# An attention and FFN kernel: the third bank of a score group to VectorE, and two row blocks in FFN at once

## The chip, the cores and the metric

The kernel runs on one core of one Trainium2 chip. The metric is device time in microseconds, from a median of runs. A core has five engines with queues of their own: TensorE (PE; its weight loads are shown apart as PEld), VectorE (DVE), ScalarE (ACT), GpSimd (POOL) and SyncE (SP), which issues the transfers here. An engine works its queue off in order; what must wait for another engine waits on a semaphore. TensorE writes to PSUM, which has eight banks of 128 x 512 float32 values.

## What is computed

Two identical layers, each an attention part and an FFN part, over 2048 rows of 448 values. There are 16 heads of 28 values.

```python
x = A_x
for layer in range(2):                       # written out twice in the reference
    n = layernorm(x)                         # mean and variance over 448, eps 1e-5
    q, k, v = split(n @ wqkv)                # 16 heads, 28 values each
    p = softmax(q @ k.T * 28 ** -0.5)        # 2048 x 2048 for each head
    x = x + merge(p @ v) @ wo
    n = layernorm(x)
    h = maximum(n @ w1 + b1, 0) ** 2         # 1792 hidden values
    x = x + h @ w2 + b2
```

The exponentials are the largest part of the work outside TensorE: 2 layers x 16 heads x 2048 x 2048 values, which are 2048 tiles of 128 x 512.

## The kernel before

The Python code holds a small planner: each stream of work yields operations with an engine, an estimated duration and what they depend on, and the planner decides the order in which every engine's instructions are issued. So a change of a rule in it moves instructions everywhere. The parts that matter here follow.

Scores are made in groups of three tiles. A group has a PSUM tile of three banks ("sc", two buffers, so six banks). The other two banks of PSUM ("m") are shared by everything else: a fourth score tile of a group, the projections, the transposes, both FFN products, and attention times values.

```python
ps_sc = ctx.enter_context(tc.tile_pool(name="ps_sc", bufs=2, space=bass.MemoryType.PSUM))
ps_m = [ctx.enter_context(tc.tile_pool(name=f"ps_m{i}", bufs=1, space=bass.MemoryType.PSUM)) for i in range(2)]
```

ScalarE does the exponential of a whole group in one instruction, and gives the group's PSUM tile back when that has ended:

```python
pt = gbuf[gi]["pt"] = ptp.tile([P, 3 * 512], DT.bfloat16, name="pt")
nc.scalar.activation(out=pt[:, 0:n], in_=gbuf[gi]["sc"][:, 0:n], func=AF.Exp,
                     scale=float(np.log(2.0)) * 2.0 ** -FRAC)
```

Some groups have a fourth tile, in a shared bank. Its exponential is computed on VectorE, in six instructions: a first one that adds, clamps and converts to integers, and so empties the bank; then the fraction's polynomial and the power of two, from SBUF:

```python
nc.vector.tensor_scalar(out=box["i"], in0=two(src), scalar1=EXP_BIAS,
                        scalar2=EXP_LOW, op0=ALU.add, op1=ALU.max)          # empties the bank
...  # cut: three scalar_tensor_tensor for the polynomial, one tensor_scalar for the power
nc.vector.scalar_tensor_tensor(out=box["two"](pd), in0=box["h"], scalar=b0,
                               in1=box["e"].bitcast(DT.bfloat16), op0=ALU.add, op1=ALU.mult)
```

Whether a group gets a fourth tile is decided when it is issued. The last condition of `apart` asks for a free shared bank:

```python
if pl.load(SPAN, "DVE") > (BB if ... else BUSY):        # cut: VectorE too full in the last 12 us
    return None
near = p_next[0] is not None and e_now[0] >= p_next[0] - NEAR_U
want[0] = sum(r.when() is not None and r.when() <= now for r in R_m) < 1 + near
return None if want[0] else j
```

TensorE repeats score matmuls where there is room before the next work, to stay busy (line 753 holds both the first making and the repeats):

```python
short = (HOT if len(units) - at[0] > ENDU else HOTE) - pl.load(HWIN)
...  # cut
for i in list(range(4)) * (again + 1):
    for k, (pi, kb, r, hh) in enumerate(us):
        nc.tensor.matmul(dst[k][:, i * nt * P:(i + 1) * nt * P], lhsT=K_sb[l][rows, g, ...], rhs=Q_sb[rows, g, ...], ...)
```

When all four head groups of a row block (256 rows; the last one of layer 1 is two of 128) are done, a chain takes it through the projection with `wo`, the addition to `x`, layer normalization, the two FFN products with relu and square between them, and, in layer 0, on to the keys, values and queries of layer 1. In layer 0, one row block at a time may hold hidden activations; they lie in a pool of seven buffers:

```python
hp = ctx.enter_context(tc.tile_pool(name="hp", bufs=NFC // 2))     # 7
R_h = [Res(1), Res(2)]                                             # row blocks with activations, by layer

def hidden(i):
    if l == 0:
        return hp.tile([P, QB], DT.bfloat16, name="h")
    c = NFC * QR * (own_h.turn % 2) + QB * i
    return V_sb[0][:, :, :, :].rearrange("p t h r -> p (t h r)")[:, c:c + QB]
```

Of the kernel before, what the change touches and what calls it, by code (L numbers as in the profile page):

```python
# [11 lines left out]
DT = mybir.dt  # L12
AF = mybir.ActivationFunctionType
ALU = mybir.AluOpType
# [20 lines left out]
DCLK = 0.2  # L35
OWN = 2
HALF = 320
BB = 0.95
TURNS = 1
ENDU = 100  # L40
HOTE = 0.8
# [5 lines left out]
GATE = [None, None, ('Q', 0, 0, 0), ('Q', 0, 0, 0), ('s', 8), ('s', 8), ('s', 8), ('s', 8)]  # L47
EARLY = 2
AHEAD = (range(0, 4), range(0, 4), range(0, 4))
SLACK = 0.6  # L50
WINDOW = 2.8
C_PRIO = 1.5
V_PRIO = 6.0
# [19 lines left out]
HOLD = 5  # L73
HOLD1 = 7
SOON = 0.6
NL = 0
NLP = 3.8
STOP = 80
# [34 lines left out]
class Planner:  # L113
# [3 lines left out]
    def __init__(self):  # L117
        self.clock = {"PE": 0.0, "ACT": 0.0, "DVE": 0.0, "POOL": 0.0, "DMA": 0.0, "-": 0.0}
        self.mode = None
        self.tok = {}  # L120
        self.streams = []
        self.past = {"PE": [], "DVE": []}
        self.turns = lambda: False

    def load(self, span, eng="PE"):

# [33 lines left out]
    def run(self):  # L160
        while self.streams:
            cands = []
            for st in self.streams:
                s, e = self.earliest(st[2]) if st[2] is not None else (None, None)
                if s is not None:
                    cands.append((s, st[0](s) if callable(st[0]) else st[0], e, st))
            assert cands, "no stream can go on"
            known = cands

            due = next((c[3][2].ready for c in cands if c[1] == 0), None)  # L170
            if due is None:
                due = next((c[0] + c[3][2].dur + LAT["ACT"] for c in cands if c[1] == 1), None)
            if due is not None:
                ok = [c for c in cands if c[2] != "PE" or c[1] == 0 or c[0] + c[3][2].dur <= due + SLACK]
                cands = ok or cands
            s, _, e, st = min(cands, key=lambda c: (max(c[3][2].ready, self.clock[c[2]]) if c[2] == "PE" and self.turns() else c[0], c[1]))
            o = st[2]
            o.eng = (e,)
            if o.acq:
                o.res = min((r for r in (o.acq() if callable(o.acq) else o.acq) if r.when() is not None), key=lambda r: r.when())  # L180
                o.turn = len(o.res.rel)
                o.res.rel.append(None)
            o.start, o.end = s, s + o.dur
            if e == "PE":
                o.room = min([c[0] for c in known if c[2] == "PE" and c[3] is not st] or [1e9]) - o.end
            if o.fn:
                o.fn(e)
            o.end += o.more
            self.clock[e] = o.end - (OVER if e == "DVE" and o.dur > 0.1 else 0.0)
            if e == "PE":  # L190
                self.mode = o.mode
            if e in self.past:
                self.past[e] = [p for p in self.past[e] if p[1] > s - 40.0] + [(s, max(s, self.clock[e]))]
            for a in o.rel:
                a.got.append(o.end + o.lat + LAT[e])
                if len(a.got) == a.need:
                    a.res.rel[a.turn] = max(a.got)
            for key in o.sets:
                self.tok[key] = o
            st[2] = next(st[1], None)  # L200
            if st[2] is None:
                self.streams.remove(st)
# [3 lines left out]
def kernel(  # L206
# [28 lines left out]
    const = ctx.enter_context(tc.tile_pool(name="const", bufs=1))  # L235
    ptp = ctx.enter_context(tc.tile_pool(name="ptp", bufs=NPT))
    xtp = ctx.enter_context(tc.tile_pool(name="xtp", bufs=3))
    hp = ctx.enter_context(tc.tile_pool(name="hp", bufs=NFC // 2))
    rp = ctx.enter_context(tc.tile_pool(name="rp", bufs=2))
    vp = ctx.enter_context(tc.tile_pool(name="vp", bufs=1))  # L240
    osp = ctx.enter_context(tc.tile_pool(name="osp", bufs=NOS))
# [7 lines left out]
    pl = Planner()  # L249
    R_sc, R_m, R_pt = Res(2), (Res(1), Res(1)), Res(NPT)  # L250
    R_r, R_xt, R_os, R_xn, R_on, R_rec = Res(2), Res(3), Res(NOS), Res(2), Res(2), Res(2)
    R_h = [Res(1), Res(2)]

    R_v = (Res(1), Res(1))


    R_pd = [*[Res(1) for _ in range(5)], Res(NFC // 2), *[Res(1) for _ in range(2)]]


    x_sb = const.tile([P, NTB, D], DT.bfloat16, name="x_sb")  # L260
# [61 lines left out]
    def late_setup():  # L322
# [14 lines left out]
        yield Op("POOL", 0.2, lambda e: nc.gpsimd.memset(ones[:], 1.0))  # L337
        yield Op("POOL", 0.2, lambda e: nc.gpsimd.memset(one0[:], 0.0))
        yield Op("POOL", 0.2, lambda e: nc.gpsimd.memset(one0[0:1, :], 1.0))
        yield Op("POOL", 0.8, lambda e: nc.gpsimd.memset(V_sb[1][:, 0:12, :, DH:DHP], 1.0))  # L340

    def loads():
        kb = 1024
# [47 lines left out]
    def spare(n):  # L391


        def f():
            if s_left and (want[0] or p_next[0] is not None and e_now[0] >= p_next[0] - (NEAR if n < 8 else FAR)):
                return R_m if all(r.when() is not None for r in R_m) else ()
            return pools_now()
        return f

    p_next = [None]  # L400
    e_now = [0, 0]
    want = [False]

    def engs_now(early=False):
        return ("ACT", "DVE") if (early and ("s", AEND) not in pl.tok) or len(s_left) == 0 else ("DVE",)

    s_left = [True]
    pl.turns = lambda: TURNS == 2 or TURNS == 1 and len(s_left) == 0

    def moments():  # L410
# [139 lines left out]
    def qkv(l, t0, nt, xnT, own_xt, ends, early=False):  # L550
# [13 lines left out]
        def values():  # L564
            nonlocal last
            for tb in range(t0, t0 + nt):
                if l == 1 and tb >= 12:
                    yield Op("POOL", 0.2, lambda e, tb=tb: nc.gpsimd.memset(V_sb[1][:, tb, :, DH:DHP], 1.0))
                def evv(e, t, tb=tb):
                    o = V_sb[l][:, tb, :, 0:DH]  # L570
# [86 lines left out]

    taken = set()
    held = [0]

    def sets_of(unit):

# [3 lines left out]
            return R_v if 2 <= qb <= 6 else R_v[:1]  # L666
        return R_v

    def apart(i, now, us):


        want[0] = False
        if len(units) - i < STOP or not LEAD <= len(gbuf) <= LAST:
            return None
        l, qb = passes[units[i][0]][:2]
        if not any(r.when() is not None and r.when() <= now + SOON for r in sets_of(units[i])):
            return None
        j = i
        if i + LAG > ends_at[units[i][0]]:
# [11 lines left out]
            return None  # L691
        if pl.load(SPAN, "DVE") > (BB if l == 0 and qb == len(blocks[0]) - 1 or l == 1 and units[i][0] < bridged else BUSY):
            return None
        near = p_next[0] is not None and e_now[0] >= p_next[0] - NEAR_U
        want[0] = sum(r.when() is not None and r.when() <= now for r in R_m) < 1 + near
        return None if want[0] else j

    def ahead(n):

# [8 lines left out]
    def s_stream():  # L708
        while at[0] < len(units):
# [5 lines left out]
            def fn(e, gi=gi, us=us, js=js):  # L715
                sc = ps_sc.tile([P, 3 * 512], DT.float32, name="sc", tag="sc")
                gbuf[gi]["sc"] = sc
                dst = [sc[:, k * 512:k * 512 + 512] for k in range(len(us))]
                at[0] = js[-1] + 1
                rest = ahead(1)  # L720
                at[0] = rest[0] if rest else len(units)
                j = apart(at[0], o.start, us) if rest else None
                if j is not None:
                    us = us + [units[j]]
                    taken.add(j)
                    held[0] += 1
                    rest = ahead(1)
                    at[0] = rest[0] if rest else len(units)
                    x = gbuf[gi]["x"] = Op("PE", 0.0, None)
                    x.res = min((r for r in R_m if r.when() is not None), key=lambda r: r.when())  # L730
                    x.turn = len(x.res.rel)
                    x.res.rel.append(None)
                    dst.append(bank(x, "mt"))
                    pl.spawn(C_PRIO, a_unit(gi, x, dst[-1], us[-1], passes[us[0][0]][0]))
                for k, (pi, kb, r, hh) in enumerate(us):
                    where.setdefault((pi, kb), []).append((gi, k, hh))
                    if len(where[pi, kb]) == G:
                        pl.tok["u", pi, kb] = o
# [74 lines left out]
    def a_unit(gi, x, src, unit, l):  # L813
# [2 lines left out]
        box = {}  # L816

        def take(e):
            box["i"], box["h"], box["e"], two = set_of(c.res, l)
            box["two"] = two  # L820
            halves = box["i"].bitcast(DT.uint16).rearrange("p a (n t) -> p a n t", t=2)
            box["f"] = halves[:, :, :, 0]
            box["n"] = box["i"].bitcast(DT.int16).rearrange("p a (n t) -> p a n t", t=2)[:, :, :, 1]
            nc.vector.tensor_scalar(out=box["i"], in0=two(src), scalar1=EXP_BIAS,  # L824
                                    scalar2=EXP_LOW, op0=ALU.add, op1=ALU.max)
# [182 lines left out]
    def chain(l, qb):  # L1008
# [16 lines left out]
        hacts = []  # L1025

        def hidden(i):
            if l == 0:
                return hp.tile([P, QB], DT.bfloat16, name="h")

            c = NFC * QR * (own_h.turn % 2) + QB * i
            return V_sb[0][:, :, :, :].rearrange("p t h r -> p (t h r)")[:, c:c + QB]
        for f0 in range(0, NFC, pack):
            fcs = range(f0, min(f0 + pack, NFC))
            w = len(fcs) * n
# [6 lines left out]
                else:  # L1042
                    nc.vector.tensor_scalar(out=r[:, 0:w], in0=t[:, 0:w], scalar1=0.0, scalar2=None, op0=ALU.max)  # L1043
            def square(e, b=b, w=w, f0=f0):
                r = b["r"]
                b["h"] = h = hidden(f0 // pack)
                nc.vector.tensor_tensor(out=h[:, 0:w], in0=r[:, 0:w], in1=r[:, 0:w], op=ALU.mult)

            def then(o, b=b, square=square):
                b["s"] = Op("DVE", 0.42, square, deps=[o], rel=o)  # L1050
# [3 lines left out]
                 for i, fc in enumerate(fcs)],  # L1054
                relu, 0.70, [*ends, ("w1",)], True, post=[then], acq=R_r)
            for i in range(len(fcs)):
                hacts.append((b, i * n, b["s"]))
        yield Op("DVE", 0.0, None, deps=[o], rel=own_xt)
        mv = moments()
        for j in range(nt):  # L1060
# [3 lines left out]
            for lo, hi in halves:  # L1064
                def store(e, tb=tb, lo=lo, hi=hi):
                    nc.sync.dma_start(out=out_view[:, tb, lo:hi], in_=x_sb[:, tb, lo:hi])
                a = yield from mm_tile(
                    [(0, hi - lo, [(one0[:, :], b2w[:, lo:hi])]
                      + [(lambda b=b, c=c: b["h"][:, c + j * P:c + (j + 1) * P], w2[:, fc, lo:hi], *([s] if own_deps else [])) for fc, (b, c, s) in enumerate(hacts)])],
                    add_to_x(tb, lo, hi), 0.15 + (hi - lo) / 950, [*([] if own_deps else [hacts[-1][2]]), ("w2",), ("b2",)],  # L1070
                    post=[(lambda a, j=j: stats(mv, t0, j, [a])) if l == 0 else
                          (lambda a, store=store: Op("DMA", 0.5, store, deps=[a]))])
# [70 lines left out]
```

The softmax here doesn't subtract the row's maximum and nothing guards it: scores larger than these inputs give would overflow.

## Time and profile before

| what | value |
|---|---|
| device time, median of 3 runs | 911.71 us (909.61 to 911.81) |
| span of the profiled execution | 908.4 us |
| granted clock of TensorE, mean | 0.996 |
| exponentials on ScalarE (line 771) | 648 |
| score matmuls and repeats (line 753) | 6352 into "sc", 384 into shared banks |

How to read the lines of the profile that are shown later: a group of instructions has its line, engine, operation, what it writes and reads, shapes and number; after the first bar its busy time and the mean length of one in ns; after the second the idle time of the engine just before them and what ended most of it ("<-PE sc L753" is TensorE's line 753 writing "sc"). A line of waits has who waited for whom, the total in us, how often, and the longest. A line of windows has the stretch, its length, busy time with number of instructions of PE, PEld, DVE, ACT and POOL, the granted clock, and the share and rate of transfers. A line of a timeline has start and length in us, engine, line, operation, shapes, number, and in brackets the idle time before it. Lengths of instructions that follow each other closely overlap, so the distance between two ends is the better measure of what one costs.

### The profile page before, as it was taken

How to read it: one execution, taken by the hardware profiler on the slowest of the kernel's cores; microseconds unless marked ns; L12 is line 12 of the kernel's file. 1: busy time of each engine (PE TensorE's matmuls, PEld its weight loads, DVE VectorE, ACT ScalarE, POOL GpSimd, SP SyncE). 2: the span in 40 equal slices, each digit the busy share in tenths (PEclk: the TensorE clock that was granted, in tenths of full speed). 3: DMA queues.
4: the chain of work that ended last, by engine and by line, in shares of the span. 5: the costliest groups of instructions: out<-in, count | busy, mean ns of one | idle time of the engine just before them, and what ended most of it. 6: DMA issues, size and time to landing. Idle time of an engine off the chain costs nothing.

```text
span 908.4 us, 30788 instructions
## 1 busy us (share of the span) xinstructions
PE 837.1 (92%) x13730; PEld 481.4 (53%) x13730; DVE 738.4 (81%) x1511; ACT 882.5 (97%) x668; POOL 42.6 (5%) x89
## 2 busy tenths in 40 slices
PE   8999989999999999999998999988989999999898
PEld 4555545455555545555455455554554455555666
DVE  7745588899898989989989684889898997887854
ACT  6999998999999999999999999999999999999994
POOL 5100000000000000000100000001000000000000
PEclk9999998999999999999999999999999999999999
DMA  7200010000000000000000000011000000000000
GB/s 228 67 3 2 2 37 22 13 10 15 14 9 14 14 9 14 14 9 8 1 3 2 2 3 1 3 39 39 17 15 25 24 9 24 19 14 24 17 18 13
DMA packets 32993, 18.54 MB, mean 20 GB/s; under 512 B 17498, under 2 KB 32411, under 8 KB 32860
## 3 DMA queue, kind: packets, MB, share of 16 engines
q1 hardware_dynamic: 32860, 16.58, 6.3%
q8 instruction: 107, 1.75, 0.8%
q14 instruction: 26, 0.21, 0.1%
HBM read 14.26 MB, written 2.07 MB: 18 GB/s over the span
## 4 chain that ended last, share of the span: by engine, by line
ACT 56%; PE 23%; issue 12%; DVE 6%; DMA 3%; POOL 0%; SPq 0%; ACTq 0%; DVEq 0%
ACT pt L771 56%; PE mt L525 9%; PE sc L753 7%; PE oT L911 4%; DMA dn<-oT_sb 3%; PE sc L525 1%; DVE v_h L839 1%; PE mt L1094 1%; DVE K_sb L839 1%; DVE st L418 1%; DVE xn L491 0%; PE mt L753 0%; PE tp L464 0%; DVE dn L977 0%; DVE oT_sb L935 0%
## 5 line engine op out<-in xcount | busy, mean ns | idle before, releaser
L771 ACT ACTIVATE pt<-sc 128x1536 bf16<-128x1536 f32 x648 | 871.9, 1604 | 5.5 <-PE sc L753 3.4
L753 PE MATMUL sc<-Q_sb,K_sb 32*128 32x256 bf16 (+1 forms) x6352 | 335.2, 265 | 54.2 <-ACT pt L771 51.2
L753 PEld LDWEIGHTS <-K_sb 32*128 32x128 bf16 x6736 | 171.7, 92 | 226.8 <-issue 218.5
L911 PE MATMUL oT<-pt,V_sb 128*32 128x256 bf16 (+1 forms) x4132 | 149.6, 269 | 0.3 <-DVE xnT L476 0.3
L525 PE MATMUL mt<-xnT,w 128*128 128x256 bf16 (+1 forms) x912 | 116.2, 270 | 3.0 <-DVE oT_sb L933 1.3
L911 PEld LDWEIGHTS <-V_sb 128*32 128x32 bf16 x4352 | 94.2, 97 | 43.0 <-issue 38.6
L839 DVE SCALAR_TENSOR_TENSOR K_sb<-K_sb 128x512 f32<-128x512 uint16 x144 | 98.4, 683 | 1.5
L525 PEld LDWEIGHTS <-w 128*128 128x128 bf16 x952 | 80.2, 97 | 34.1 <-issue 25.5
L1043 DVE TENSOR_SCALAR r<-mt 128x512 bf16<-128x512 f32 x105 | 72.0, 685 | 13.9 <-PE mt L525 13.0
L839 DVE SCALAR_TENSOR_TENSOR v_h<-v_h,v_i 128x512 f32<-128x512 f32 x116 | 79.0, 681 | 0.3
L753 PE MATMUL mt<-Q_sb,K_sb 32*128 32x256 bf16 (+1 forms) x384 | 58.3, 265 | 0.9 <-DVE x_sb L1005 0.9
L1005 DVE TENSOR_TENSOR x_sb<-x_sb,mt 128x448 bf16<-128x448 bf16 (+1 forms) x62 | 37.6, 607 | 17.7 <-PE mt L525 17.7
L525 PE MATMUL mt<-w,h 128*128 128x448 bf16 x224 | 51.9, 354 | 0.0
L1094 PE MATMUL mt<-xn,ident 128*128 128x448 bf16 x140 | 48.5, 359 | 2.5 <-DVE xn L491 1.3
L440 POOL TENSOR_TENSOR ve<-mv,eps_t 128x2 f32<-128x2 f32 (+1 forms) x34 | 9.2, 270 | 851.9 <-DVE mv L419 851.9
L824 DVE TENSOR_SCALAR v_i<-mt 128x512 int32<-128x512 f32 x58 | 39.7, 684 | 11.3 <-PE mt L753 11.3
L824 DVE TENSOR_SCALAR K_sb<-mt 128x512 int32<-128x512 f32 x48 | 32.9, 686 | 17.3 <-PE mt L753 17.1
L525 PE MATMUL mt<-w,V_sb 128*128 128x448 bf16 (+1 forms) x210 | 46.7, 346 | 0.0
L418 DVE BATCH_NORM_STATS2 st<-x_sb 128x6 f32<-128x448 bf16 x64 | 39.6, 618 | 0.9 <-DMA x_sb<-in_A_x_dram 0.7
L839 DVE SCALAR_TENSOR_TENSOR v_h<-v_i 128x512 f32<-128x512 uint16 x58 | 39.5, 682 | 0.3
L933 DVE COPY oT_sb<-oT 128x256 f32<-128x256 f32 (+1 forms) x48 | 19.1, 399 | 24.2 <-PE oT L911 23.9
L491 DVE TENSOR_SCALAR xn<-x_sb,mv,rstd 128x448 bf16<-128x448 bf16 x64 | 25.4, 418 | 9.5 <-POOL rstd L441 9.2
(98 smaller groups left out, 746.8 us busy)
## 6 DMA issues: line engine op xcount, KB each, us to landing
rec<-scr SPq DMA_DIRECT2D x56, 128.0 KB
x_sb<-in_A_x_dram SPq DMA_DIRECT2D x8, 224.0 KB
out_dram<-x_sb SPq DMA_DIRECT2D x15, 112.0 KB
w<-in_B_w_dram SPq DMA_DIRECT2D x1, 1568.0 KB
w<-in_B_w_dram SPq DMA_DIRECT2D x1, 1344.0 KB
dn<-oT_sb SPq DMA_DIRECT2D x56, 4.0 KB
scr<-dn SPq DMA_DIRECT2D x56, 4.0 KB
V_sb<-in_A_wqkv_dram SPq DMA_DIRECT2D x1, 672.0 KB
```

Of the source, the lines that this page charges most:

```text
L418: nc.vector.bn_stats(out=st[:, :], in_=x_sb[:, t0 + j, :])
L491: nc.vector.tensor_scalar(out=xn[:, 0:D], in0=x_sb[:, t0 + j, :], scalar1=mv[0][:, j, 0:1], scalar2=ln[j], op0=ALU.subtract, op1=ALU.mult)
L525: nc.tensor.matmul(box["t"][:, c0:c0 + n], lhsT=lhsT() if callable(lhsT) else lhsT, rhs=rhs, start=a, stop=b)
L753: nc.tensor.matmul(dst[k][:, i * nt * P:(i + 1) * nt * P], lhsT=K_sb[l][rows, g, (kb + i) * P:(kb + i + 1) * P], rhs=Q_sb[rows, g, t0 * P: ...
L771: nc.scalar.activation(out=pt[:, 0:n], in_=gbuf[gi]["sc"][:, 0:n], func=AF.Exp, scale=float(np.log(2.0)) * 2.0 ** -FRAC)
L824: nc.vector.tensor_scalar(out=box["i"], in0=two(src), scalar1=EXP_BIAS, scalar2=EXP_LOW, op0=ALU.add, op1=ALU.max)
L839: nc.vector.scalar_tensor_tensor(out=box["h"], in0=box["f"] if begin else box["h"], scalar=b, in1=box["f"], op0=ALU.add, op1=ALU.mult)
L911: nc.tensor.matmul(box["t"][DHP * hh:DHP * hh + DHP, 0:n], lhsT=V_sb[l][:, kb + i, 4 * g + hh, :], rhs=p[:, c0:c0 + n], start=begin and kb ...
L933: nc.vector.tensor_copy(out=dst, in_=src)
L1005: nc.vector.tensor_tensor(out=x_sb[:, tb, lo:hi], in0=x_sb[:, tb, lo:hi], in1=t[:, 0:hi - lo], op=ALU.add)
L1043: nc.vector.tensor_scalar(out=r[:, 0:w], in0=t[:, 0:w], scalar1=0.0, scalar2=None, op0=ALU.max)
L1094: nc.tensor.matmul(t[:, 0:D], lhsT=ident[:, :], rhs=xns[0][:, 0:D], start=True, stop=True)
```

## The change

Two things. First, where VectorE could take a tile but no shared bank is free, the group's own third bank is given to it: the group then has two tiles for ScalarE (1024 wide) and a third one, of its own PSUM tile, for VectorE. That PSUM tile is given back when both engines have read it. For this, a set of VectorE's scratch buffers must be free at once. Second, in layer 0 two row blocks may hold hidden activations at the same time. Six of a block's seven pieces now go where the same rows' keys, queries and values of layer 1 will be written later, so the pool shrinks from seven buffers to three. The columns of ones in `V_sb[1]` are therefore written by GpSimd as each row block's values are made, rather than at the start.

With it, the rule that held the shared banks back for a waiting fourth tile (`want`) is removed, and two numbers are set anew: how full VectorE may be around the change of layers (`BB`), and how far other work of TensorE may run past the time at which the next score group is due (`SLACK`, now shortened after a group with two tiles).

The core of the diff, with cuts marked:

```diff
-BB = 0.95
+BB = 0.85
-SLACK = 0.6
+SLACK = 0.5
+NHP = 3
+THIRD = 1
...
-    hp = ctx.enter_context(tc.tile_pool(name="hp", bufs=NFC // 2))
+    hp = ctx.enter_context(tc.tile_pool(name="hp", bufs=NHP))
...
-    R_h = [Res(1), Res(2)]
+    R_h = [Res(2), Res(2)]
...
-        yield Op("POOL", 0.8, lambda e: nc.gpsimd.memset(V_sb[1][:, 0:12, :, DH:DHP], 1.0))
...
-            if s_left and (want[0] or p_next[0] is not None and e_now[0] >= p_next[0] - (NEAR if n < 8 else FAR)):
+            if s_left and (p_next[0] is not None and e_now[0] >= p_next[0] - (NEAR if n < 8 else FAR)):
...
+    def slack():
+        n = gbuf[-2]["n"] if len(gbuf) > 1 else 3
+        return SLACK - (3 - n) * 512 / 1200
...
-                if l == 1 and tb >= 12:
+                if l == 1:
                     yield Op("POOL", 0.2, lambda e, tb=tb: nc.gpsimd.memset(V_sb[1][:, tb, :, DH:DHP], 1.0))
...
-                j = apart(at[0], o.start, us) if rest else None
-                if j is not None:
-                    us = us + [units[j]]
+                own, j = True, None
+                if bank_free(o.start) and next_at(js[-1] + 1):
+                    j = apart(at[0], o.start, us)
+                elif len(us) == 3 and THIRD:
+                    own = False
+                    next_at(js[1] + 1)
+                    j = apart(at[0], o.start, us[:2], 0.0)
+                if j is None:
+                    next_at(js[-1] + 1)
+                else:
+                    if not own:
+                        us, ks = us[:2], ks[:2]
+                        gbuf[gi]["n"] = 2
+                    us, ks = us + [units[j]], ks + [3]
...
+                    if own:
                         (a shared bank is taken, as before)
+                    else:
+                        x = gbuf[gi]["x"] = o
+                        o.need = 2
...
         def hidden(i):
+            flat = lambda a: a.rearrange("p (f q) -> p f q", q=n)
+            if l == 0 and i < 4:
+                return (K_sb[1], Q_sb)[i // 2][:, 2 * (i % 2):2 * (i % 2) + 2, t0 * P:t0 * P + n]
+            if l == 0 and i < 6:
+                return flat(V_sb[1][:, t0:t0 + nt, :, :].rearrange("p t h r -> p (t h r)")[:, QB * (i - 4):QB * (i - 3)])
             if l == 0:
-                return hp.tile([P, QB], DT.bfloat16, name="h")
+                return flat(hp.tile([P, QB], DT.bfloat16, name="h")[:, :])
```

## The prediction

> **What bounds the kernel now.** I read the page's parts in this order: busy times, slices, chain, groups; then the waits of ScalarE, the windows, and the timelines of two places. The first part and the chain say which engine sets the time.
>
> ```profile
> PE 837.1 (92%) x13730; PEld 481.4 (53%) x13730; DVE 738.4 (81%) x1511; ACT 882.5 (97%) x668; POOL 42.6 (5%) x89
> ...
> ACT 56%; PE 23%; issue 12%; DVE 6%; DMA 3%; POOL 0%; SPq 0%; ACTq 0%; DVEq 0%
> ...
> L771 ACT ACTIVATE pt<-sc 128x1536 bf16<-128x1536 f32 x648 | 871.9, 1604 | 5.5 <-PE sc L753 3.4
> L753 PE MATMUL sc<-Q_sb,K_sb 32*128 32x256 bf16 (+1 forms) x6352 | 335.2, 265 | 54.2 <-ACT pt L771 51.2
> ```
>
> The exponentials of line 771 fill 871.9 of 908.4 us, and ScalarE stood idle before them for 5.5 us in all. TensorE, busy 92%, waited 51.2 us *for* them, so its share is filler: line 753 repeats score matmuls when there is room. ScalarE is the bound from about 11 us, when the first exponential starts, to 892 us, when the last one ends. Head and tail are bound otherwise. So only three things can move the end: the length of ScalarE's queue, its gaps, and the tail.
>
> Read one by one from the timeline of ScalarE, the ends of two successive 1536-wide exponentials lie 1.342 us apart (median of 647), and the single 512-wide one took 0.490 us from the end before it. So an element costs (1.342 - 0.490) / 1024 = 0.83 ns, and an instruction 0.490 - 512 x 0.00083 = 0.064 us on top. A 1024-wide one should then take 0.916 us (my estimate from these two).
>
> The gaps are in the next answers. ScalarE's largest waits:
>
> ```profile
> ACT r L1041 <- PE sc L525: 5.6, 2, 4.4
> ACT wk L371 <- DMA V_sb<-in_A_wqkv_dram: 4.1, 1, 4.1
> ACT pt L771 <- PE sc L753: 3.4, 5, 1.1
> ACT pt L771 <- PE mt L753: 1.5, 3, 1.1
> ```
>
> The first belongs to the tail and the second to the head. The last two are the whole loss between exponentials that the waits name; summed from the ends, delays over 15 ns come to 7.6 us. About 1.2 us lies at 25.6 us (layer 0's start), and most of the rest in one place, which the windows show:
>
> ```profile
> 100.00:135.00 35.00, 30.91 (x567) 17.26 (x565) 25.73 (x55) 35.00 (x27) 0.00 (x0) 1.00 0.09 22
> 135.00:147.00 12.00, 10.12 (x166) 5.67 (x168) 10.67 (x25) 9.05 (x7) 1.30 (x2) 0.72 0.12 36
> 147.00:250.00 103.00, 96.53 (x1525) 55.34 (x1513) 91.65 (x188) 102.93 (x78) 4.37 (x8) 1.00 0.05 13
> ```
>
> The columns after the stretch are its length, busy time of PE, PEld, DVE, ACT and POOL, then the granted clock. Only in 135 to 147 us is the clock 0.72, and only there is ScalarE not full: 9.05 of 12 us. The timeline of TensorE at that place:
>
> ```profile
> 135.15 0.28 PE L753 MATMUL sc<-Q_sb,K_sb 32*128 32x256 bf16 x3
> 136.36 0.26 PE L753 MATMUL mt<-Q_sb,K_sb 32*128 32x256 bf16 x1 [0.93 <-DVE x_sb L1005]
> ...
> 138.48 1.34 PE L753 MATMUL sc<-Q_sb,K_sb 32*128 32x256 bf16 x18 [0.95 <-ACT pt L771]
> ```
>
> A score group whose fourth tile goes into a shared bank had to wait 0.93 us until VectorE had emptied that bank; two idle stretches of nearly 1 us then followed each other, the clock fell to half, and four exponentials came late by 1.17, 0.25, 1.20 and 0.76 us, 3.4 us together.
>
> **What the Trainium skill says.** "ScalarE: Activation LUTs", section What ACT_TABLE_LOAD costs: an ACTIVATE with immediate scale and bias takes 186 ns + 0.833 ns per element, and back-to-back ones overlap by about 93 ns. The slope agrees with the trace (0.83); the remainder, 93 ns, is above the 64 ns here, and I use the trace. "TensorE: Matmul & The Clock Gate", section What's actually happening: the gate passes half or all clock pulses depending on how busy the array was recently; the trace agrees, with a clock of 0.72 in the stretch above and 1.00 elsewhere. "PSUM — Partial Sum Buffer", section Specifications: ScalarE and VectorE read PSUM in parallel at full rate as long as they are on different banks. The change makes them read different banks of one score tile; no run yet shows that.
>
> **The change, part by part.** The counts are those of the instructions in the two built programs, engine by engine.
>
> *Exponentials.* There are 2048 score tiles of 128x512. Before, 106 went to VectorE and 1942 = 647 x 3 + 1 to ScalarE. After, 120 go to VectorE: 45 still through a shared bank, 75 through the third bank of a group. ScalarE keeps 1928 = 592 x 3 + 76 x 2. Its time is 647 x 1.342 + 0.490 = 868.8 us before, and 592 x 1.342 + 76 x 0.916 = 864.1 us after: **4.7 us less**, on the path. This is small because most of the 75 take the place of tiles that had a shared bank, and because each adds an instruction's 0.064 us.
>
> *VectorE.* One tile is six instructions: 686 (L824), three of 682 (L839), 416 (L834) and 681 ns (L845), 3.83 us. Durations of all VectorE instructions sum to 826 us where the engine is busy for 738, so overlap takes off a tenth: 3.4 us. Fourteen more are 48 us: from 738 to about 786 us, 87%. They land mainly where VectorE had room (ScalarE time 450 to 800 us, where I count 56 tiles in place of 46). The windows have VectorE at about 91% in 250 to 450 us with ScalarE at 100%, so that load is known to be bearable. Cost on the path: none by itself.
>
> *TensorE.* 634 fewer score matmuls, all repeats. Nothing on the path.
>
> *Two row blocks in FFN, activations in their later keys' places.* The squares are as many as before and go to other addresses; GpSimd's one memset of twelve row blocks becomes twelve small ones, on an engine that is busy 5%. No cost. Its use is that the work of a row block of layer 0 can be spread over more time.
>
> *The tail.* The programs differ after the last score matmul. Before, TensorE still has 112 matmuls of 128 columns for the first FFN product, 32 for attention times values, and 19 of 448 columns. After, it has the same 112, but 64 and 34: one and a half FFN outputs (28 in place of 14 of 448) are left over, and the transposes of row block 14 too. At 190 ns a 448-wide matmul (its usual distance), the 15 additional ones are 2.9 us, and the 32 of attention, 14 ns apart, 0.4 us. In the trace before, the last row block's attention, projection and normalization are a chain of waits, up to 899.3 us, and TensorE fills it with row block 14's FFN. After, row block 14 starts its FFN only during that chain, so half of its output (7 x 0.19 = 1.3 us) goes ahead of the last block's and the rest (1.3 us) after it. The final addition takes 0.62 rather than 0.29 us. **About 3.0 us more**, on the path.
>
> *The gaps.* If the half clock does not come back, 3.4 us are saved. The same pile-up (four heads finish together, VectorE waits for small transfers, shared banks wait for VectorE) is in the new order of instructions, so I give it even odds: -1.7 us. For 75 groups whose score tile is released by both engines I add 1.5 us of new waits.
>
> Sum: 911.7 - 4.7 + 3.0 - 1.7 + 1.5 = 909.8; as the third bank removes the wait for a shared bank at exactly such places, I lean a little lower and say **909.0 us**.
>
> **Rivals.** *First: the third bank becomes the wait.* A score tile is free only when VectorE has taken its third bank. From the end of the score matmuls to the need of the same buffer there are about 0.916 + 1.342 us of exponentials, and VectorE's queue in front of it is one or two instructions of 0.7 us; with priority given to it I expect few waits. Were VectorE late by 0.1 us on average, 75 of them would make 7.5 us, and the change would lose: 914 to 917. For it: VectorE grows to 87%, and it runs in order behind waits for transfers (5.0 us for "dn"). Against it: TensorE waited for VectorE only 10 us or so in the whole run.
>
> *Second: the clock.* TensorE has 634 fewer repeats to keep it busy, and each fall of the clock costs some 3.4 us. None would give about 906, two about 912.
>
> *Third: the tail is hidden after all.* If the leftover outputs fit into waits of the last chain, the 3.0 us vanish: about 906.
>
> **Range and chances.** Best case: tail hidden, no fall of the clock: 911.7 - 4.7 - 3.4 = 903.6. Bad case: tail as counted, clock as before, 5 us of new waits: 915. So 904 to 915 holds it 8 times in 10. A change of 2% is 18 us, four times what ScalarE gains; I see no path to it downward (0.02), and upward only if VectorE falls behind over long stretches (0.03).
>
> **What would show it.** Right: exponentials in two widths, 592 and 76, the narrow ones 0.92 us apart; VectorE busy about 786 us; last exponential some 5 to 8 us earlier than 891.8, and then a longer tail, 19 to 20 us instead of 16.6. Rival one would show as "PE sc" waiting for VectorE's first step on the score tile. Rival two as windows with a clock under 1. I would be wrong by the largest amount if VectorE, fuller now, stalls behind transfers, so that score tiles come free late in many places.

## The result and the profile after

The changed kernel takes **945.39 us** (median of 4 runs, 942.67 to 945.99) against 910.66 us for the kernel before on the same chip: a ratio of 1.0378, 95% interval 1.0348 to 1.0408. It is 3.8% slower; the prediction was 909.0 us with a range of 904 to 915.

From the page of the changed kernel, the busy times, the chain, and the group of exponentials (its line is 799 now, that of the scores 781, and VectorE's first step on a tile is line 853):

```profile
PE 844.7 (89%) x13089; PEld 469.1 (50%) x13089; DVE 782.5 (83%) x1595; ACT 886.2 (94%) x688; POOL 42.9 (5%) x100
...
ACT 46%; PE 21%; DVE 18%; issue 13%; POOL 1%; DMA 1%; POOLq 0%; ACTq 0%; SPq 0%
...
L799 ACT ACTIVATE pt<-sc 128x1536 bf16<-128x1536 f32 (+1 forms) x668 | 875.5, 1449 | 33.7 <-PE sc L781 15.9
L781 PE MATMUL sc<-Q_sb,K_sb 32*128 32x256 bf16 (+1 forms) x5966 | 328.1, 266 | 72.1 <-ACT pt L799 52.9
```

ScalarE is busy for nearly the same time, but stood idle before its exponentials for 33.7 us where it had been 5.5. VectorE's share of the chain that ended last went from 6% to 18%. The waits of ScalarE for its exponentials say on whom:

```profile
ACT pt L799 <- PE sc L781: 15.9, 31, 1.4
ACT pt L799 <- DVE K_sb L853: 9.7, 16, 1.4
ACT pt L799 <- DVE v_i L853: 6.3, 11, 1.4
```

The last two are new in kind. An exponential waits, 27 times, for VectorE's *first step on a score tile* (`K_sb` and `v_i` are here two of VectorE's scratch buffers). It needs no result of that step. And VectorE waits for the exponentials, whose result its first step does not need either. Here are two lines near the top of VectorE's waits, and then the first three of TensorE's:

```profile
DVE K_sb L853 <- ACT pt L799: 15.1, 16, 1.3
DVE v_i L853 <- ACT pt L799: 13.6, 13, 1.5
```

```profile
PE sc L781 <- ACT pt L799: 52.9, 123, 1.1
PE sc L781 <- DVE K_sb L853: 8.9, 15, 1.0
PE sc L781 <- DVE v_i L853: 6.1, 10, 1.2
```

The built program shows where this comes from. These are the waits written into the instructions for the first third-bank group and for the third one; the offset 1024 is the third bank, the exponential reads banks one and two:

```
VectorE  v_i  <- sc_1823 (offset 1024)   waits for TensorE's scores
ScalarE  pt   <- sc_1823 (offset 0)      waits for VectorE's v_i <- sc_1823
...
ScalarE  pt   <- sc_3065 (offset 0)      waits for TensorE's scores
VectorE  K_sb <- sc_3065 (offset 1024)   waits for ScalarE's pt <- sc_3065
```

All 75 groups have such a wait, 43 of the first kind and 32 of the second. The layer that records the kernel puts two engines that *read* the same PSUM tile in the order of their issue, though they read different banks. The planner, which decided that order, counts them as parallel. One place in the timeline has both kinds in a row:

```profile
319.75 2.42 ACT L799 ACTIVATE pt<-sc 128x1536 bf16<-128x1536 f32 x2
...
322.21 0.69 DVE L853 TENSOR_SCALAR K_sb<-sc 128x512 int32<-128x512 f32 x1 [0.98 <-ACT pt L799]
322.82 0.68 DVE L853 TENSOR_SCALAR v_i<-sc 128x512 int32<-128x512 f32 x1
322.95 0.40 PE L781 MATMUL sc<-Q_sb,K_sb 32*128 32x256 bf16 x6 [0.70 <-DVE K_sb L853]
...
323.59 3.71 ACT L799 ACTIVATE pt<-sc 128x1024 bf16<-128x1024 f32 x3 [1.42 <-DVE v_i L853]
```

A line of several instructions gives the shape of the first: the two that start at 319.75 are a wide exponential and a narrow one. VectorE was idle for 0.98 us until that narrow one had ended (322.17), then took its group's third bank. Only after it could it take the next group's. That group's exponential needed no more scores (TensorE made none between 321.71 and 322.95), but had to wait for VectorE's step: ScalarE, the bound, was idle for 1.42 us. TensorE meanwhile waited 0.70 us for the first tile to come free. The clock fell to half at 324.8 us for 3.4 us; there were four such stretches between head and tail, 17 us together.

The account in spans (944.2 - 908.4 = 35.8 us):

| part | before | after | difference |
|---|---|---|---|
| exponentials, by number and distance of ends | 868.8 | 864.1 | -4.7 |
| delays between exponentials over 15 ns | 7.6 | 44.6 | +37.0 |
| end of the last exponential to the end | 16.6 | 20.2 | +3.6 |
| sum | | | +35.9 |

The delays are more than the 33.7 us of idle time: an exponential of 1536 that starts after a pause ends 1.45 us after its start, where in a row the ends lie 1.342 us apart.

### The profile page after: what moved, and what is told of

Its sections match the earlier page's. It is cut to its first block, busy times and chain, and to the rows that moved or that the text cites. A ratio compares the mean times of both kernels' runs of the same rounds, so it can differ in the third digit from the quotient of the medians.

```text
span 944.2 us, 29595 instructions
## 1 busy us (share of the span) xinstructions
PE 844.7 (89%) x13089; PEld 469.1 (50%) x13089; DVE 782.5 (83%) x1595; ACT 886.2 (94%) x688; POOL 42.9 (5%) x100
## 4 chain that ended last, share of the span: by engine, by line
ACT 46%; PE 21%; DVE 18%; issue 13%; POOL 1%; DMA 1%; POOLq 0%; ACTq 0%; SPq 0%
ACT pt L799 46%; PE mt L532 9%; PE sc L781 7%; PE oT L940 3%; DVE v_h L868 2%; DVE K_sb L868 2%; DVE K_sb L853 2%; DVE v_i L853 2%; DVE r L1077 1%; DVE v_e L863 1%; DVE st L425 1%; PE mt L1128 1%; DVE xn L498 1%; DVE V_sb L874 1%; DVE x_sb L1034 1%
## 5 line engine op out<-in xcount | busy, mean ns | idle before, releaser
L799 ACT ACTIVATE pt<-sc 128x1536 bf16<-128x1536 f32 (+1 forms) x668 | 875.5, 1449 | 33.7 <-PE sc L781 15.9
L781 PEld LDWEIGHTS <-K_sb 32*128 32x128 bf16 x6102 | 161.4, 92 | 249.9 <-issue 241.5
L868 DVE SCALAR_TENSOR_TENSOR K_sb<-K_sb 128x512 f32<-128x512 uint16 x165 | 112.6, 683 | 0.7 <-PE mt L532 0.2
L868 DVE SCALAR_TENSOR_TENSOR v_h<-v_h,v_i 128x512 f32<-128x512 f32 x130 | 88.7, 683 | 0.5
L532 PE MATMUL mt<-w,V_sb 128*128 128x448 bf16 (+1 forms) x288 | 68.8, 353 | 0.0
L853 DVE TENSOR_SCALAR K_sb<-sc 128x512 int32<-128x512 f32 x38 | 26.1, 688 | 18.1 <-ACT pt L799 15.1
L532 PEld LDWEIGHTS <-V_sb 128*128 128x128 bf16 x302 | 25.6, 98 | 24.9 <-issue 9.5
L853 DVE TENSOR_SCALAR v_i<-sc 128x512 int32<-128x512 f32 x37 | 25.4, 687 | 15.0 <-ACT pt L799 13.6
L498 DVE TENSOR_SCALAR xn<-x_sb,mv,rstd 128x448 bf16<-128x448 bf16 x64 | 25.3, 419 | 12.7 <-POOL rstd L448 12.4
L532 PE MATMUL mt<-xnT,wq 128*128 128x256 bf16 x248 | 35.2, 281 | 0.0
L532 PE MATMUL mt<-xnT,wk 128*128 128x256 bf16 x240 | 33.3, 276 | 0.1
```

The source lines that it names most:

```text
L498: nc.vector.tensor_scalar(out=xn[:, 0:D], in0=x_sb[:, t0 + j, :], scalar1=mv[0][:, j, 0:1], scalar2=ln[j], op0=ALU.subtract, op1=ALU.mult)
L532: nc.tensor.matmul(box["t"][:, c0:c0 + n], lhsT=lhsT() if callable(lhsT) else lhsT, rhs=rhs, start=a, stop=b)
L868: nc.vector.scalar_tensor_tensor(out=box["h"], in0=box["f"] if begin else box["h"], scalar=b, in1=box["f"], op0=ALU.add, op1=ALU.mult)
```

## The experiments

Theory A: the order of the two readers is the loss. Theory B: VectorE is too full and takes its banks late. Theory C: the second row block in FFN, or the changed rules about shared banks, is the loss.

### The order of the two readers left away

```diff
+    def apart_reads(gi, late):
+        g = gbuf[gi]
+        if g["n"] == 2 and "ie" in g and "it" in g:
+            first = g["it"] if late is g["ie"] else g["ie"]
+            ...
+            tc.declare_no_dep(ins(late), ins(first), reason="they read different banks of one tile")
```

It is called after each exponential and after each first step of VectorE. Each engine's instructions stand in the same order as in the changed kernel.

> The changed kernel with every instruction in the same place; only the semaphore waits between a group's 1024-wide exponential and VectorE's first step on the same score tile are left away (they read different banks; all other waits stay). Theory A (the two readers of one PSUM tile are put in order by semaphores, and this is the loss): delays between exponentials fall from 44.6 us to some 10 to 15, time 908 to 916 us. Theory B (VectorE is too full and takes its banks late, so score tiles come free late): the waits only move to TensorE's score matmuls, time 930 us or more. Theory C (the loss is in the two row blocks or the rules about shared banks): about 945 us.

Measured: **905.63 us**, ratio to before 0.9934 (0.9909 to 0.9959); 39.8 us come back, more than theory A expected, and it is faster than both kernels. The profiled execution is the longest of its four (908.82 us); in it the delays between exponentials sum to 6.0 us. The groups of exponentials by form, in the changed kernel and then here:

```profile
L799 ACT ACTIVATE pt<-sc 128x1536 bf16<-128x1536 f32 x592 | 808.5, 1500 | 17.3 <-PE sc L781 15.9 <-PE oT L940 0.2
L799 ACT ACTIVATE pt<-sc 128x1024 bf16<-128x1024 f32 x76 | 78.0, 1047 | 16.4 <-DVE K_sb L853 9.7 <-DVE v_i L853 6.3
```

```profile
L799 ACT ACTIVATE pt<-sc 128x1536 bf16<-128x1536 f32 x592 | 813.4, 1603 | 4.0 <-PE sc L781 3.4 <-PE oT L949 0.2
L799 ACT ACTIVATE pt<-sc 128x1024 bf16<-128x1024 f32 x76 | 87.2, 1195 | 0.0
```

The narrow ones had 16.4 us of idle time before them and now have none; the wide ones, whose tiles came free late, go from 17.3 to 4.0. In the built program none of the 75 waits is left. This is theory A. Theory B falls: VectorE is as full as before (779.0 us busy) and tiles come free in time.

### No third bank

```diff
-THIRD = 1
+THIRD = 0
```

> The changed kernel with THIRD = 0: no group gives its third bank away; 94 tiles to VectorE through shared banks, 651 exponentials of 1536 and one of 512 (874.1 us at 1.342 and 0.490). Two row blocks in FFN, the removed rule and the two numbers stay. Theories A and B: delays back to about 8 us, time 912 to 918 us, slower than before by ScalarE's 5.3 us. Theory C: 935 us or more.

Measured: 912.76 us, ratio 1.0020 (1.0005 to 1.0036). Delays sum to 3.0 us and the last exponential ends at 893.4 us. The loss goes with the third bank; what is left of the change costs 1.8 us, with twelve tiles fewer on VectorE than before. Theory C falls for the kernel as a whole.

### The third bank with one row block in FFN

```diff
-NHP = 3
+NHP = 7
-    R_h = [Res(2), Res(2)]
+    R_h = [Res(1), Res(2)]
     (all hidden activations of layer 0 in the pool of seven again)
```

> The third bank (72 groups, 122 tiles to VectorE in all) with one row block of layer 0 in FFN at a time and seven buffers, as before. Theories A and B: the delays stay at about 40 us, time 938 to 948 us. Theory C: most of the loss goes with the second row block, time below 920 us.

Measured: 950.63 us, ratio 1.0425 (1.0405 to 1.0445), a little above the expected range. The waits of ScalarE show an item that the changed kernel doesn't have, first in the list:

```profile
ACT pt L800 <- PE mt L782: 12.7, 1, 12.7
ACT r L1078 <- PE mt L533: 11.8, 4, 7.7
```

It is one wait of 12.7 us, at 601.9 us: scores of layer 1 that need the keys of the last row block, which comes late through its FFN. A later run tests whether the single row block makes it.

### The two directions of the order, one at a time

```diff
-        if g["n"] == 2 and "ie" in g and "it" in g:
+        if g["n"] == 2 and "ie" in g and "it" in g and late is g["ie"]:    # or: late is g["it"]
```

The first frees the 43 exponentials that come second, the other the 32 first steps that come second.

> The changed kernel, same order; the wait is left away only in the 43 groups where the exponential is issued after VectorE's first step and waits for it. The 32 waits of VectorE for the exponential stay. In the changed kernel ScalarE waited 16.0 us for that first step directly, and TensorE 15.0 us for score tiles released late by it. If the two directions cost alike, about half of the 40 us comes back: 922 to 928 us. If only VectorE's waiting (and the late release after it) matters: 935 or more. If only ScalarE's: 908 to 912.

> The other half: the wait is left away only in the 32 groups where VectorE's first step is issued after the exponential. The 43 waits of the exponential stay. Equal costs: 922 to 928 us; the sum of what this and the run before recover should be near 40 us if the two add up.

Measured: 922.65 us (ratio 1.0133, 1.0109 to 1.0156) and 917.72 us (1.0083, 1.0064 to 1.0103). The first is inside the range for equal costs, the second below it. They recover 22.7 and 27.7 us, 50.4 together, where both at once recover 39.8. So they don't add up, against the second run's condition. Part of the surplus can be the clock: in neither of the two profiles is there a half-speed stretch between head and tail. In the changed kernel the delays from the start of each of the four stretches to 3 us after its end sum to 7.5 us, and either run can recover these, but both together only once. How far the losses also feed each other directly, as at 322 us, is not separated. As both runs stay 12 to 17 us above the first one with the clock full, the order costs time without the clock. The 32 are worth more than the 43, and each more than half alone. With the 43 freed, what is left is late tiles, in TensorE's waits:

```profile
PE sc L781 <- ACT pt L799: 36.6, 95, 0.9
PE sc L781 <- DVE K_sb L861: 8.6, 15, 1.0
PE sc L781 <- DVE v_i L861: 5.5, 9, 1.2
```

With the 32 freed, what is left is short waits of ScalarE for the first step, none over 0.5 us:

```profile
ACT pt L799 <- DVE K_sb L861: 4.2, 14, 0.4
ACT pt L799 <- DVE v_i L861: 3.4, 10, 0.5
```

### One row block in FFN, without the order

The edit of the third run on top of that of the first.

> Third bank without the reader order, but one row block of layer 0 in FFN at a time (72 groups with a 1024-wide exponential, 594 with 1536). The same with the order had one delay of 12.8 us at the change of layers. If that delay comes from the single row block, and not from the order: about 905.6 + 12 + 3 for a longer tail (49 in place of 34 matmuls of 448 columns after the last scores), 917 to 922 us. If it came from the order: 906 to 910.

Measured: 921.68 us, ratio 1.0122 (1.0105 to 1.0138), inside the first range. In the timeline of ScalarE the delay is there at the change of layers, with nothing of the order in play, and the tail is 25.5 us:

```profile
569.23 4.39 ACT L800 ACTIVATE pt<-sc 128x1536 bf16<-128x1536 f32 x3
584.99 2.36 ACT L800 ACTIVATE pt<-sc 128x1536 bf16<-128x1536 f32 x2 [11.38 <-PE mt L782]
```

So with the third bank in use, the second row block is worth 16 us (921.68 - 905.63): a delay of 11.4 us and a tail longer by 5.3 us. The kernel before, with one row block and no third bank, has no such delay. When TensorE makes the last row block's first keys for layer 1 shows one side of it; in order, here, in the first run and in the kernel before:

```profile
581.58 1.26 PE L533 MATMUL mt<-xnT,wk 128*128 128x256 bf16 x8 [0.78 <-DVE xnT L484]
```

```profile
568.51 1.05 PE L532 MATMUL mt<-xnT,wk 128*128 128x256 bf16 x8
```

```profile
571.66 1.03 PE L525 MATMUL mt<-xnT,wk 128*128 128x256 bf16 x8
```

The keys come 10 us later than in the kernel before, and the scores are ahead of it: by 575 us ScalarE had finished or VectorE had taken 1321 of the 2048 tiles, against 1308. Why the row block itself is later is not shown.

### Numbers of the planner, without the order

Four variants of the first run's kernel were made to shorten its tail and to see what the change of layers depends on.

```diff
-BB = 0.85
-SLACK = 0.5
-STOP = 80
+BB = 0.95        # short tail, and BB alone
+SLACK = 0.6      # short tail, and SLACK with STOP
+STOP = 140       # short tail, STOP alone, and SLACK with STOP
```

> The kernel without the reader order, with the old numbers BB 0.95 and SLACK 0.6, and no fourth or third-bank tiles in the last 140 score tiles instead of 80. Exponentials take the same 864.1 us; after the last scores 19 matmuls of 448 columns and 116 of 128 are left instead of 34 and 136, 4.4 us of TensorE's time. If the tail counts as the prediction counted it: 900 to 903 us. If the tail is set by its chain of waits alone: 904 to 907.

> The kernel without the reader order, BB 0.95 in place of 0.85 and nothing else: VectorE may be 95% full around the change of layers. The run with BB 0.95, SLACK 0.6 and STOP 140 had one delay of 13.5 us at 587 us. If BB makes it: the delay is back and the time about 905.6 + 11, 914 to 920 us. If SLACK or STOP made it: 902 to 907.

> The kernel without the reader order, BB 0.85 and SLACK 0.5, but VectorE takes no tiles among the last 140 instead of 80. Exponentials 865.8 us (1.7 more); TensorE's work after the last scores 15.0 instead of 17.1 us by count. If the tail follows that work and the change of layers keeps its order: 904 to 907 us, the same as without; a delay of over 10 us at 587 us would mean 915 or more.

> As the run before with SLACK 0.6: exponentials 865.8 us (1.7 more than without the reader order), TensorE's work after the last scores 12.9 instead of 17.1 us by count. If the tail follows that work (4 us, as it did in the run with BB 0.95, 16.2 against 20.2 us) and there is no delay at the change of layers: 901 to 905 us, below both kernels. With such a delay: 913 or more.

| variant | time (us) | ratio to before (95%) | largest delay between exponentials (us) | last exponential to end (us) |
|---|---|---|---|---|
| BB 0.95, SLACK 0.6, STOP 140 | 916.39 | 1.0063 (1.0046 to 1.0081) | 13.5 at 587 | 16.2 |
| BB 0.95 | 918.88 | 1.0095 (1.0077 to 1.0113) | 13.2 at 587 | 21.5 |
| STOP 140 | 907.87 | 0.9969 (0.9957 to 0.9980) | 1.7 at 19 | 20.4 |
| SLACK 0.6, STOP 140 | 911.79 | 1.0015 (1.0008 to 1.0023) | 2.4 at 579 | 16.9 |

The first was a miss: the tail did become 4 us shorter, as counted, but the delay at the change of layers came back. The second shows that `BB` does that, alone: with VectorE allowed to be 95% full there, the last row block's first keys are made at 583.4 us in place of 568.5. The third is a miss: the time is 0.9 us above the expected range, and the tail is as long as without it. TensorE has less left, but the 14 matmuls of the other row block's output now stand wholly after the last block's. The fourth, also a miss, lies between its two ranges: it has the shorter tail, and loses it to more delays (10.0 us in place of 6.0), also at the change of layers. None is better than the first run's kernel; the third comes near it, with intervals that touch.

## Why the prediction was wrong

*The exponentials: right.* 592 and 76 instructions, and 4.7 us less. In the run without the order the narrow ones' ends lie 0.917 us after the ends before them (median); the estimate was 0.916. One reason given for the small gain is wrong: not each of the 75 adds an instruction; there are 20 more in all (668 for 648), 1.3 us.

*VectorE's load: right, and harmless.* 782.5 us busy; 786 was expected. Without the order, the same load leaves ScalarE at 6.0 us of delays.

*The tail: right, a little short.* 20.2 us, 3.6 more than before; 19 to 20, about 3.0 more, was forecast, for the reason given: seven of row block 14's matmuls stand before the last block's output and seven after it, at the end of TensorE's timeline.

```profile
935.17 1.49 PE L532 MATMUL mt<-w,V_sb 128*128 128x448 bf16 x7
...
939.37 1.49 PE L532 MATMUL mt<-w,V_sb 128*128 128x448 bf16 x7
```

*The half clock.* At 139 us it did not come back (it had even odds, so this proves nothing), but four other stretches came, 17 us where there had been 6.8. So no gain of 1.7 us.

*"For 75 groups whose score tile is released by both engines I add 1.5 us of new waits": this step failed.* The delays grew by 37.0 us. It rested on the reading that ScalarE and VectorE would work on different banks of one tile at once, which the Trainium skill's "PSUM — Partial Sum Buffer", section Specifications, says the hardware can do. It can: without the order, all 75 pairs overlap in time, 34 of them for over 0.6 us; in these 34 the exponentials keep their distance of 0.917 us. VectorE's first steps on a third bank take 681 to 682 ns in the median, as those on a shared bank (682 to 688). But the built program doesn't allow it. The prediction counted the built program's instructions and their order, not the waits attached to them, where the order of the two readers is written.

*Rival one named the right place and the wrong reason.* It expected a late VectorE, 0.1 us in the mean, and score matmuls waiting; it gave 914 to 917. What it missed is that an exponential itself could wait for VectorE, and VectorE for an exponential. The prediction gave a slowdown of over 2% a chance of 0.03, through a VectorE that falls behind; it came through the order instead. Rival two, the clock, came as a consequence: with the same few repeats but without the order, the profile has one half-speed stretch between head and tail instead of four. Its 906 and 912 us don't follow from the sum, where half a fall is in the 909.0: none would give 907.3, two 914.1. Rival three, a hidden tail, was wrong; the tail is not shorter than counted.

*What the second row block is for was undersized.* The prediction said that it spreads work over more time, at no cost and with no number. It is worth 16 us with the third bank in use: without it ScalarE comes to the scores of layer 1 that need the last row block's keys before these are there, and the tail is longer.

## What to carry to other kernels

When a change lets a second engine read a tile, look at the semaphore waits of exactly those instructions in the built program: reads of one tile may be put in order, whatever the hardware could do, and then a helper engine becomes a link of the bound engine's chain. Allowed to run apart, the same instructions in the same order went from 3.8% slower to 0.7% faster. A planner that doesn't know of a wait doesn't hide it; and a gain on the bound engine can be lost at the next place that waits for the slowest chain, here the change of layers.

## What the runs showed of the hardware

ScalarE and VectorE reading different banks of one three-bank tile at the same time cost each other nothing that can be seen: in the 34 pairs that overlap for over 0.6 us, the exponentials' ends lie 0.914 to 0.918 us after the ends before them and VectorE's steps take 0.675 to 0.692 us.

Short idle times that come close together can be followed by a fall of TensorE's clock: in the kernel before, two of 0.93 and 0.95 us within 3.1 us. But the same idle times don't always bring it. Here is one place of the same instructions in two runs, the one without the order and the one with the 32 freed:

```profile
854.26 0.40 PE L781 MATMUL sc<-Q_sb,K_sb 32*128 32x128 bf16 x12 [0.93 <-ACT pt L799]
855.60 1.47 PE L781 MATMUL sc<-Q_sb,K_sb 32*128 32x128 bf16 x36 [0.65 <-ACT pt L799]
```

```profile
864.71 0.40 PE L781 MATMUL sc<-Q_sb,K_sb 32*128 32x128 bf16 x12 [0.93 <-ACT pt L799]
866.05 0.85 PE L781 MATMUL sc<-Q_sb,K_sb 32*128 32x128 bf16 x36 [0.65 <-ACT pt L799]
```

In the first run the clock is at half from 855.4 us on, for 6.8 us, and 36 matmuls take 1.47 us. In the second it stays full, and they take 0.85 us. What decides is not shown here. The half-speed stretches between head and tail were 3.4 or 6.8 us long in all seven profiles that have any.
